# Linear branch of a gated attention mix: transpositions by transposing DMAs in place of TensorE and VectorE, and 107 vector packs spread anew

## The chip, the cores and the metric

The kernel runs on one core of a Trainium2 chip. The metric is the time of one execution in microseconds, measured on the device. The engines are TensorE (PE in the profile), VectorE (DVE), ScalarE (ACT), GpSimd (POOL) and SyncE (SP), which issues most DMAs.

## The reference

Two branches read the same x (2048 tokens, 512 features, bf16, 32 heads of 16) and are mixed by a gate of one number per token.

```python
x = A_x
g = sigmoid((x * gate_w).sum(-1, keepdims=True))
# A: softmax attention
q, k, v = heads(x @ A_wqkv)
a = heads_back(softmax(q @ k.T * 16**-0.5) @ v) @ A_wo
# B: linear attention with softmax features ("hedgehog")
q, k, v = heads(x @ B_wqkv)
pq, pk = q @ w_phi, k @ w_phi                      # 16 x 16 per head
phi_q = concat([softmax(pq), softmax(-pq)], -1)    # 32 features
phi_k = concat([softmax(pk), softmax(-pk)], -1)
kv, z = phi_k.T @ v, phi_k.sum(tokens)
b = heads_back((phi_q @ kv) / (phi_q @ z + 1e-6)) @ B_wo
return g * a + (1 - g) * b
```

## The kernel before

**Units and packs.** The attention branch is cut into 2048 units: one head, one block of 128 keys, one chunk of 512 queries. Four heads make a pack, 16 packs (all key blocks, kt 0 to 15) a group, 32 groups the branch: 512 packs. Scores of a unit are one matmul on a quarter of TensorE's rows (`_scores`, L839) into a PSUM bank. For most units ScalarE takes the exponential (`_exp`, L891), in instructions of 3 and 2 units alternately, out of a ring of five banks. The values follow as matmuls on quarters of TensorE's columns (`_values`, L958), accumulated over a group in one further bank. `_norm` then transposes the group's sums and divides.

**Vector packs.** Some packs ("away") do not go to ScalarE. For these VectorE builds the exponential from bit patterns: four instructions from PSUM (`_vector_bits`, L777, tile va) and three shifted copies (`_vector_terms`, L795, tile vp), so that such a pack has 16 value matmuls instead of 4. `PACKS` says how many packs of each group are away, `CHOICE` which.

**Linear branch.** `_b_fuse` multiplies the projection weights by the feature weights once for K (s=1) and once for Q (s=0): it transposes the weights into WT (TensorE L1050, copy L1055), and the product (L1068) goes back into WB (L1073). `_b_pair` makes the features of two tiles of 128 tokens: projection, a chain of VectorE instructions (L1099 to L1131) and one exponential on ScalarE (L1124). For K they are summed into kv (`_b_kv`, L1148). For Q, `_b_phit` transposes them into phiT: 8 transposes of 128x128 (L1189) and one copy (L1196) a tile. `_b_num` multiplies by kv (L1213), divides (L1220 to L1225, tile nb, two buffers) and transposes the result (L1235, copy L1241) into onTB, which shares its memory with WT. `_b_out` and `_out` add both branches' output products (L1252, L1285) in one bank, and the rows are stored. The branch works in four chunks of 512 tokens.

**The order.** Nothing is issued in program order. `Plan.order` is a list scheduler: every operation has a cost, a latency, a priority (mostly a due time counted in packs) and sometimes a release time. It takes what can start first, the lowest priority among equals, and writes a fixed queue for each engine. Banks outside the ring are handed out as they come free. The constants `K0, SK` and `Q0, SQ` are due times of the K and Q halves in packs (first one, and step per tile); `LEAD`, `FIRST` say how far ahead of its pack a vector pack is begun; `AHEAD` how late other matmuls may run before scores. At low load `pad` and `filler` add matmuls on zeros (L965). On the chip each engine then runs its queue in order, and an operation waits on semaphores for what it needs. DMAs on SP have a semaphore each and also run in the order's sequence.

Of the kernel before, what the change touches and what calls it, by code (L numbers as in the profile page):

```python
# [7 lines left out]
ALU = mybir.AluOpType  # L8
AX = mybir.AxisListType

P = 128
# [32 lines left out]
class Op:  # L44
    def __init__(self, eng, fn, cost, name, prio, rel, kind, lat):
        self.eng, self.fn, self.cost, self.name = eng, fn, cost, name
        self.prio, self.rel, self.kind, self.lat = prio, rel, kind, lat
        self.deps = []
        self.users = []
        self.left = 0  # L50
        self.need = False
        self.acquire = None
        self.release = None
        self.sem = None
        self.start = self.end = None
        self.on_commit = None
        self.array = 0.0
        self.filler = 0
        self.slack = None
        self.fits = True  # L60
        self.pad = False
        self.want = None
        self.tiles = []
        self.filled = 0
# [39 lines left out]
class Plan:  # L104
# [10 lines left out]
    def __init__(self):  # L115
        self.ops = []
        self.now = -1
        self.free_banks = []
        self.keep = None
        self.open = None  # L120
        self.pad = None
        self.grow, self.grow_at = None, 1e9
# [30 lines left out]
    def _bank_for(self, o):  # L153

        free = self.free_banks
        if o.want is not None:
            return [b for b in free if b[0] == o.want]
        if self.now >= self.grow_at - (20 if o.kind == "col" else 2):
            free = [b for b in free if b[0] != self.grow]
        return free if len(free) > (self.keep is not None and self.keep is not o.acquire) else []  # L160

    def order(self):
# [14 lines left out]
        while left:  # L177
# [82 lines left out]
            if o.on_commit:  # L260
                o.on_commit(o)
# [5 lines left out]
        return queues  # L267

# [82 lines left out]
class _Kernel:  # L351
    RING, WIDER = 5, 99999
# [3 lines left out]
    AHEAD = 0.56  # L356
    NB, NVA, NVP, LEAD = 4, 4, 6, 11
    FIRST = 6
    KT0, KTS, NKT = 1, 3, 5
    KEEP, EARLY = 14, 2.5  # L360
# [13 lines left out]
    def build(self):  # L374
        with ExitStack() as ctx:
# [4 lines left out]
            p.grow = self.RING  # L380
# [279 lines left out]
    def _proj_q(self, qc, cp, bank=None):  # L660
        n = qc * 4 + cp
        due = 32 * n - 14.0 if n else -2.0
# [72 lines left out]
    PACKS = (2, 0, 4, 3, 2, 3, 5, 1, 5, 4, 3, 3, 5, 5, 4, 2, 3, 5, 3, 2, 4, 4, 3, 3, 2, 5, 2, 3, 3, 5, 4, 3)  # L735
    CHOICE = ((), (7,), (4, 10), (1, 7, 13), (1, 4, 10, 13), (1, 4, 7, 10, 13))

    def _plan_vector(self):

        self.away = []  # L740
        for g, n in enumerate(self.PACKS):
            self.away += [self.NT * g + k for k in self.CHOICE[n]]
        self.hooks = {}
        hook = lambda p, fn: self.hooks.setdefault(max(0, p), []).append(fn)
        for k, p in enumerate(self.away):
            due = max(p - self.LEAD, self.FIRST)
            past = lambda n: self.away[n] + 1 if n >= 0 else 0
            hook(max(int(due) - 4, past(k - self.NVA)), lambda k=k, p=p, due=due: self._vector_bits(k, p, due))
            hook(max(p - 2, past(k - 1 - (self.NVP - len(SHIFTS)) // len(SHIFTS))), lambda k=k, p=p: self._vector_terms(k, p))
# [4 lines left out]
    def _value_copies(self):  # L754
        end = self.KT0 + self.KTS * (self.NKT - 1) + 1
        self.o_vc = [self.plan.op("DVE", lambda e, cp=cp: e.tensor_scalar(
            self.vc[:, cp], self.V[:, self.KT0:end:self.KTS, cp, :], FACTOR, None, op0=ALU.mult), 0.27,
# [3 lines left out]
    def _vector_bits(self, number, pack, due):  # L761
# [6 lines left out]
        step = 1.0  # L768
        parts = []
        for j in range(self.NB):  # L770
# [8 lines left out]
                op0=ALU.mult, op1=ALU.add), self.c_dve(512), deps=[m] + b.readers, name="v_bits", prio=at - 40,  # L779
# [4 lines left out]
    def _vector_terms(self, number, pack):  # L784
# [5 lines left out]
        for k, (shift, scaled) in enumerate(SHIFTS):  # L790
            x = len(SHIFTS) * number + k
            if x >= self.NVP:
# [3 lines left out]
                         0.07 + n * 0.00026, reads=[b_a], writes=[b], name="v_term", prio=pack - 2)  # L796
            self.terms[pack].append((t, b, scaled))

    def _attention(self):
# [9 lines left out]
        plan.grow_at = self.mine[self.WIDER] / 4 if self.WIDER < len(self.mine) else 1e9  # L809
# [8 lines left out]
        while a < len(self.mine):  # L818
            b = min(a + (2 if a < self.WIDER and len(self.exps) % 2 else 3), len(self.mine))
# [30 lines left out]
    def _ring(self, a):  # L850

        return a % self.RING if a < self.WIDER else (a - self.WIDER) % (self.RING + 1)

    def _qk(self, a, b):
# [17 lines left out]
        def commit(_):  # L872
            plan.now = max(plan.now, (units[-1] + 1) // 4)
        o.on_commit = commit
        o.tiles = [u % 4 for u in units]
        o.pad = k >= 8
        if a == self.WIDER + 3:
            o.acquire, o.want = Job(), self.RING
# [4 lines left out]
    def _exp(self, a, b):  # L883
# [10 lines left out]
        last = range(max(a, len(self.mine) - self.RING - (len(self.mine) > self.WIDER)), b)  # L894
        if last:
            o.on_commit = lambda o: plan.free_banks.extend((self._ring(x), o.end + o.lat, [o]) for x in last)
        self.exps.append(o)

    def _pv(self, p):
# [22 lines left out]
        o = self.plan.op("PE", run, 0.23, reads=[self.b_zero], deps=deps, name=f"pv{p}", prio=p + (2.5 if kt else self.EARLY), kind="col",  # L922
                         acquire=None if kt else ot, array=0.0533 * len(src))
        def commit(_):
            if kt == 0:
                plan.open, plan.keep = ot, None
            elif kt == (self.KEEP if plan.now < plan.grow_at else 99) and g + 1 < self.NPACK // NT and self.ot[g + 1].bank is None:
                plan.keep = self.ot[g + 1]
            elif kt == NT - 1:
                plan.open = None  # L930
        plan = self.plan
        o.on_commit = commit
# [7 lines left out]
    def _pv_terms(self, p):  # L940
# [3 lines left out]
        for tile, buf, scaled in self.terms.pop(p):  # L944
# [5 lines left out]
                             prio=p + 2.6, kind="col", array=0.2133)  # L950
# [23 lines left out]
    def _norm(self, qc, src, side, last, dst, b_dst, due, job, alone=False):  # L974
# [5 lines left out]
           deps=last, writes=[b_T1[side]], name="n_t1", prio=due - 8, release=job)  # L980
        if not (side or alone):
# [6 lines left out]
        op("DVE", lambda e: e.reciprocal(rinv[:, lo:hi], rinv[:, lo:hi]), 0.12 + 0.055 * n, reads=[b_rinv],  # L988
# [3 lines left out]
            rinv[:, lo:hi, :, None].to_broadcast([P, n, 16, 16]), ALU.mult), 0.05 + 0.25 * n,  # L992
# [5 lines left out]
    K0, SK, Q0, SQ = 30.0, 13.25, 226.0, 16.0  # L998

    def _branch_b(self):  # L1000
# [27 lines left out]
        for ch in range(NQC):  # L1028
            for tt in (0, 2):
# [3 lines left out]
                self._b_phit(tt, phi, 0, due + 12)  # L1033
                self._b_phit(tt + 1, phi, 1, due + 14)
# [6 lines left out]
    def _b_fuse(self, s, due):  # L1041
        op = self.plan.op
        for half in range(2):
            job = Job()
            m = None
            for c2 in range(2):
                def tr(e, c=2 * half + c2, c2=c2, job=job):
                    bank = self._bank(job).bitcast(BF16)
                    for cp in range(4):
                        ins = e.transpose(bank[:, 512 * c2 + P * cp:512 * c2 + P * cp + P],  # L1050
                                          self.WB[:, c, D * s + P * cp:D * s + P * cp + P], self.iden[:])
                    return ins
                m = op("PE", tr, 4 * self.c_pe(128), reads=[self.b_WB, self.b_iden], deps=[m] + self.b_WT.readers,
                       name="wtr", prio=due, rel=due - 10, acquire=None if c2 else job)
            o = op("DVE", lambda e, half=half, job=job: e.tensor_copy(  # L1055
                self.WT[:, :, 256 * half:256 * half + 256].rearrange("p q (c m) -> p c q m", c=2),
                self._bank(job).bitcast(BF16).rearrange("p (c q m) -> p c q m", c=2, q=4)), 0.62, deps=[m], name="wtr_ev",
                prio=due, release=job)
            if half:
                self.b_WT.writers, self.b_WT.readers = [first, o], []  # L1060
            first = o
# [120 lines left out]
    def _b_phit(self, tt, slot, k, due):  # L1182
        op = self.plan.op
        job = Job()

        def tr(e):
            bank = self._bank(job).bitcast(BF16)
            for gg in range(8):
                ins = e.transpose(bank[:, P * gg:P * gg + P], self.bq[:, slot, k, P * gg:P * gg + P], self.iden[:])  # L1189
            return ins  # L1190
        if tt == 0:
            self.phit_war = list(self.b_phiT.readers)
            self.b_phiT.writers, self.b_phiT.readers = [], []
        m = op("PE", tr, 8 * self.c_pe(128), reads=[self.b_bq[slot], self.b_iden], deps=self.phit_war, name="phit",
               prio=due, acquire=job)
        o = op("DVE", lambda e: e.tensor_copy(  # L1196
            self.phiT[:, :, tt * TOK:tt * TOK + TOK],
            self._bank(job).bitcast(BF16).rearrange("p (g q) -> p g q", g=8)), 0.605, deps=[m] + self.phit_war,
            name="phit_ev", prio=due, release=job)
        self.b_phiT.writers.append(o)  # L1200

    def _b_num(self, t, due):
# [27 lines left out]
        job = Job()  # L1230

        def tr(e):
            bank = self._bank(job).bitcast(BF16)
            for pr in range(4):
                ins = e.transpose(bank[:, P * pr:P * pr + P], nb[:, P * pr:P * pr + P], self.iden[:])  # L1235
            return ins
        m = op("PE", tr, 4 * self.c_pe(128), reads=[b_nb, self.b_iden], name="nbt", prio=due + 1, acquire=job)
        if tt == 0:
            self.ontb_war = list(self.b_onTB.readers)
            self.b_onTB.writers, self.b_onTB.readers = [], []  # L1240
        self.b_onTB.writers.append(op("DVE", lambda e: e.tensor_copy(  # L1241
            self.onTB[:, :, tt * TOK:tt * TOK + TOK],
            self._bank(job).bitcast(BF16)[:, 0:D].rearrange("p (r q) -> p r q", q=TOK)), 0.34,
            deps=[m] + self.ontb_war, name="nbt_ev", prio=due + 1, release=job))
# [20 lines left out]
    def _out(self, qc):  # L1265
        op, NT, NQC = self.plan.op, self.NT, self.NQC
        for tt in range(4):
            t = 4 * qc + tt
            final = qc == NQC - 1
            due = max(128 * (qc + 1) + 8, self.Q0 + self.SQ * (4 * qc + 4) + 22) + 4 * tt  # L1270
# [71 lines left out]
```

## Time and profile before

| | |
|---|---|
| median of 3 runs | 791.22 us (790.95 to 792.47) |
| profiled execution | 790.92 us |
| its span, first to last instruction | 788.9 us |
| busy: TensorE | 766.6 us, 97% |
| busy: ScalarE | 768.6 us, 97% |
| busy: VectorE | 729.4 us, 92% |
| mean granted TensorE clock | 1.000 |
| DMA: moved in the span | 9.48 MB |

Busy time is the union of an engine's instructions. Matmuls are pipelined and their ends are modelled, so TensorE's share says how often it had work, not how fast it ran. In the tables, "PE" is the matmul and "PEld" its weight load; "SPq" is SP's queue of DMA issues. Durations of neighbouring instructions on VectorE and ScalarE overlap by some 0.1 us, and the chain of waits lists the distances instead.

### The profile page before, as it was taken

What the parts mean: (1) busy time and instruction counts of PE and PEld (TensorE: products, weight loads), DVE (VectorE), ACT (ScalarE), POOL (GpSimd) and SP (SyncE); (2) the same over time, 40 slices, a digit from 0 to 9 for tenths busy, and PEclk for the clock granted to TensorE, in tenths of its full rate; (3) what the DMA queues carried; (4) which work ended last, traced back from release to release, by engine and by line L of the source; (5) the groups of instructions that cost most, each with busy time, mean ns of one, the idle gap of its engine ahead of it and who ended that gap; (6) DMA issues with size and microseconds to landing.
All of it is one profiled execution on the core that took longest, in us unless ns stands there. A gap on an engine that the chain in (4) does not pass through costs nothing.

```text
span 788.9 us, 17147 instructions
## 1 busy us (share of the span) xinstructions
PE 766.6 (97%) x7506; PEld 243.9 (31%) x7506; DVE 729.4 (92%) x1325; ACT 768.6 (97%) x671; POOL 6.9 (1%) x14
## 2 busy tenths in 40 slices
PE   9999999999999999999999999999999999999998
PEld 4333333233222232222222333223332233223332
DVE  5778989898999999999999999899988999799994
ACT  5799999999999999999999999999999999999996
POOL 2000000000000000000000000000000000000000
PEclk9999999999999999999999999999999999999999
DMA  9200000000000000000000000000000000000000
GB/s 267 55 2 1 2 1 2 1 2 1 2 1 2 1 2 1 2 2 1 2 2 1 2 1 8 15 8 1 2 7 21 2 2 2 14 15 1 2 2 27
DMA packets 10857, 9.48 MB, mean 12 GB/s; under 512 B 3616, under 2 KB 10272, under 8 KB 10784
## 3 DMA queue, kind: packets, MB, share of 16 engines
q1 hardware_dynamic: 8912, 7.75, 3.2%
q8 instruction: 58, 0.95, 0.5%
q10 hardware_dynamic: 1872, 0.66, 0.3%
q14 instruction: 15, 0.12, 0.1%
HBM read 6.31 MB, written 2.10 MB: 11 GB/s over the span
## 4 chain that ended last, share of the span: by engine, by line
ACT 81%; DVE 9%; PE 9%; issue 0%
ACT ET L891 78%; ACT bq L1124 3%; DVE va L777 3%; PE ps L839 3%; DVE vp L795 2%; PE ps L958 2%; PE ps L634 1%; PE ps L688 1%; PE ps L1252 1%; PE ps L1285 0%; PE ps L594 0%; PE ps L965 0%; PE ps L609 0%; DVE xT L615 0%; DVE VB L1083 0%; DVE bq L1121 0%
## 5 line engine op out<-in xcount | busy, mean ns | idle before, releaser
L891 ACT ACTIVATE ET<-ps 128x1536 bf16<-128x1536 f32 (+1 forms) x651 | 740.5, 1327 | 11.4 <-PE ps L839 10.4
L839 PE MATMUL ps<-qT,kT 32*128 32x512 bf16 x2048 | 340.2, 384 | 12.7 <-ACT ET L891 8.7
L777 DVE TENSOR_SCALAR va<-ps 128x512 uint16<-128x512 f32 x420 | 276.5, 682 | 6.7 <-PE ps L839 5.9
L795 DVE TENSOR_SCALAR vp<-va 128x2048 uint16<-128x2048 uint16 x315 | 209.0, 686 | 1.3 <-PE ps L958 0.9
L839 PEld LDWEIGHTS ps<-qT,kT 32*128 32x128 bf16 x2048 | 83.9, 91 | 266.6 <-ACT ET L891 145.3
L958 PE MATMUL ps<-ET,V 128*32 128x512 bf16 x1628 | 158.4, 386 | 0.6 <-DVE T L979 0.3
L958 PE MATMUL ps<-vp,vc 128*32 128x512 bf16 x840 | 74.8, 384 | 0.9 <-DVE vp L795 0.9
L965 PE MATMUL ps<-kT,zero 128*32 128x512 bf16 x832 | 75.0, 386 | 0.0
L958 PEld LDWEIGHTS ps<-ET,V 128*32 128x32 bf16 x1628 | 41.3, 94 | 68.8 <-issue 57.0
L634 PE MATMUL ps<-WB,xT 128*128 128x512 bf16 x192 | 54.8, 383 | 0.6 <-DVE T L979 0.2
L958 PE MATMUL ps<-vp,V 128*32 128x512 bf16 x420 | 41.3, 384 | 0.9 <-DVE vp L795 0.9
L958 PE MATMUL ps<-va,V 128*32 128x512 bf16 x420 | 41.7, 387 | 0.0
L634 PE MATMUL ps<-xT,WA 128*128 128x512 bf16 (+1 forms) x132 | 36.8, 377 | 0.4 <-DVE va L777 0.2
L1124 ACT ACTIVATE bq<-bq 128x2048 bf16<-128x2048 bf16 x16 | 31.7, 1983 | 0.0
L958 PEld LDWEIGHTS ps<-vp,vc 128*32 128x32 bf16 x840 | 19.8, 95 | 34.3 <-issue 17.0
L965 PEld LDWEIGHTS ps<-kT,zero 128*32 128x32 bf16 x832 | 18.6, 94 | 36.2 <-issue 34.2
L979 DVE STREAM_TRANSPOSE T<-ps 128x512 f32<-128x512 f32 x32 | 22.7, 708 | 7.4 <-PE ps L958 7.3
L1099 DVE CAST bq<-ps 128x512 bf16<-128x512 f32 x32 | 21.8, 683 | 6.6 <-PE ps L634 6.6
L674 DVE TENSOR_TENSOR qT<-ps,mask 128x1024 bf16<-128x1024 f32 x15 | 18.3, 1217 | 2.8 <-PE ps L634 2.8
L634 PEld LDWEIGHTS ps<-WB,xT 128*128 128x128 bf16 x192 | 12.6, 97 | 24.8 <-issue 12.0
L1294 DVE CAST WB<-ps 128x512 bf16<-128x512 f32 x12 | 8.3, 690 | 12.6 <-PE ps L1285 11.2
L688 PE MATMUL ps<-WA,xT 128*128 128x128 bf16 x256 | 19.6, 220 | 0.0
(84 smaller groups left out, 439.6 us busy)
## 6 DMA issues: line engine op xcount, KB each, us to landing
xn<-in_A_x_dram SPq DMA_DIRECT2D x3, 512.0 KB, 7.1
WB<-in_B_wqkv_dram SPq DMA_DIRECT2D x1, 1536.0 KB, 8.8
out_dram<-WB SPq DMA_DIRECT2D x12, 128.0 KB, 1.7
WA<-in_A_wqkv_dram SPq DMA_DIRECT2D x3, 384.0 KB, 8.8
xn<-in_A_x_dram SPq DMA_DIRECT2D x2, 256.0 KB, 3.7
wphi<-in_B_w_phi_dram SPq DMA_DIRECT2D x32, 0.5 KB, 2.1
WoA<-in_A_wo_dram SPq DMA_DIRECT2D x1, 512.0 KB, 4.1
WoB<-in_B_wo_dram SPq DMA_DIRECT2D x1, 512.0 KB, 5.1
```

The lines of the kernel that those rows point to most:

```text
L634: ins = e.matmul(self._bank(job)[:, 0:n], lhs(c), rhs(c), start=(c == 0), stop=(c == 3))
L674: [lambda e, b: e.tensor_tensor(self.qT[:, s0:s0 + 2, :], b[:, None, :].to_broadcast([P, 2, QCH]), self.mask[:, :, None].to_broadcast([P, ...
L688: ins = e.matmul(self._bank(job)[:, P * tt:P * tt + P], self.xT[:, c, QCH * j + TOK * tt:QCH * j + TOK * tt + TOK], self.WA[:, 2, c, P * c ...
L777: parts.append(op("DVE", lambda e, j=j, job=job: e.tensor_scalar(self.va[:, slot, j, :], self._bank(job), SCALE * LOG2E * 128.0, (127.0 - ...
L795: self.plan.op("DVE", lambda e, t=t, shift=shift: e.tensor_scalar(flat(t), a, float(shift), None, op0=ALU.add), 0.07 + n * 0.00026, reads= ...
L839: return e.matmul(out, self.kT[32 * i:32 * i + 32, cp, kt * TOK:(kt + 1) * TOK], self.qT[32 * i:32 * i + 32, s, :], start=True, stop=True, ...
L891: o = plan.op("ACT", lambda e: e.activation(self.ET[:, a % NS:a % NS + n, :], self.ps[:, self._ring(a):self._ring(a) + n, :], ACT.Exp, sca ...
L958: ins = e.matmul(self._bank(ot)[32 * i:32 * i + 32, :], V[:, v0:v0 + 32], tile, start=(kt == 0), stop=(kt == self.NT - 1), tile_position=( ...
L965: ins = e.matmul(self._bank(ot)[32 * i:32 * i + 32, :], self.zero[:], self.kT[:, 0, 0:QCH], start=False, stop=False, tile_position=(0, 32 ...
L979: op("DVE", lambda e: e.transpose(T1[:, side].rearrange("p b s -> p (b s)"), src()), 0.635, deps=last, writes=[b_T1[side]], name="n_t1", p ...
L1099: [lambda e, b, k=k: e.tensor_copy(bq[:, k].rearrange("p (g s v) -> p g s v", g=8, s=2)[:, :, 0, :], b.rearrange("p (g v) -> p g v", g=8))],
L1124: op("ACT", lambda e: e.activation(flat, flat, ACT.Exp), self.c_act(2048) + 0.045, reads=[b], writes=[b], name="b_exp", prio=due + 1)
```

## The change

1. The three kinds of transposes of the linear branch (weights, Q's features, quotients) are done by DMAs that transpose on the way from SBUF to SBUF, all issued by SP, 8 + 16 + 16 of them. TensorE's transposes and VectorE's copies for them go, with the banks between. In the order each is entered with a cost of 0.3 us on SP and a latency (`TURN`) of 5.0 us.
2. The away packs are listed as bits per group for kt 1, 4, 7, 10, 13 (`AWAY`, 107 in place of 105). Per group they were 2 0 4 3 2 3 5 1 5 4 3 3 5 5 4 2 3 5 3 2 4 4 3 3 2 5 2 3 3 5 4 3 and are 0 2 3 3 3 3 3 3 4 4 5 2 3 4 3 4 5 3 4 3 3 5 2 3 3 4 4 4 3 3 5 4.
3. Constants of the order get other values: due times of the linear branch, lead and priorities of vector packs, of the group's transposition and of output rows. Some costs are entered anew.
4. Code that had no effect at these settings (a wider ring) goes, and callbacks become `_commit`.

```diff
-    RING, WIDER = 5, 99999
+    RING = 5
-    AHEAD = 0.56
-    NB, NVA, NVP, LEAD = 4, 4, 6, 11
-    FIRST = 6
+    AHEAD = 0.53
+    NB, NVA, NVP, LEAD = 4, 4, 6, 12.25
+    FIRST = 3
-    KEEP, EARLY = 14, 2.5
+    KEEP = 12
+    TURN = 5.0
+    STEP, BITS, TERM, PVX, NORM, QDUE, PUT = 0.85, -56.0, 4.5, -0.7, -22, -14.0, 6.95
...
-    PACKS = (2, 0, 4, 3, 2, 3, 5, 1, 5, 4, 3, 3, 5, 5, 4, 2, 3, 5, 3, 2, 4, 4, 3, 3, 2, 5, 2, 3, 3, 5, 4, 3)
-    CHOICE = ((), (7,), (4, 10), (1, 7, 13), (1, 4, 10, 13), (1, 4, 7, 10, 13))
+    AWAY = (0, 20, 25, 13, 11, 22, 22, 14, 30, 15, 31, 10, 21, 29, 13, 27, 31, 28, 29, 14, 26, 31, 5, 25, 14, 15, 15, 30, 21, 21, 31, 23)
...
-            hook(max(int(due) - 4, past(k - self.NVA)), lambda k=k, p=p, due=due: self._vector_bits(k, p, due))
+            hook(max(min(int(due) - 4, p - 2), past(k - self.NVA)), lambda k=k, p=p, due=due: self._vector_bits(k, p, due))
...
-        step = 1.0
+        step = self.STEP
...
-                op0=ALU.mult, op1=ALU.add), self.c_dve(512), deps=[m] + b.readers, name="v_bits", prio=at - 40,
+                op0=ALU.mult, op1=ALU.add), self.c_dve(512), deps=[m] + b.readers, name="v_bits", prio=at + self.BITS,
...
-                         0.07 + n * 0.00026, reads=[b_a], writes=[b], name="v_term", prio=pack - 2)
+                         0.07 + n * 0.00026, reads=[b_a], writes=[b], name="v_term", prio=pack + self.TERM)
...
-                             prio=p + 2.6, kind="col", array=0.2133)
+                             prio=p + self.PVX, kind="col", array=0.2133)
...
-           deps=last, writes=[b_T1[side]], name="n_t1", prio=due - 8, release=job)
+           deps=last, writes=[b_T1[side]], name="n_t1", prio=due + self.NORM, release=job)
...
-    K0, SK, Q0, SQ = 30.0, 13.25, 226.0, 16.0
+    K0, SK, Q0, SQ = 23.0, 12.65, 203.5, 16.8
...
     def _b_fuse(self, s, due):
...
+        war = self.b_WT.readers
+        self.b_WT.writers, self.b_WT.readers = [self._turn(
+            f"wt{s}{c}", self.WT[:, :, P * c:P * c + P], self.WB[:, c, D * s:D * s + D], [self.b_WB], war, due, due - 10)
+            for c in range(4)], []
...
+    def _turn(self, name, out, src, reads, deps, due, rel=-99):
+
+        return self.dma("SP", name, lambda e: e.dma_start_transpose(out, src), cost=0.3, reads=reads, deps=deps, prio=due,
+                        rel=rel, lat=self.TURN)
+
+    def _b_phit(self, t, slot, k, due):
+        if t % 4 == 0:
             self.phit_war = list(self.b_phiT.readers)
             self.b_phiT.writers, self.b_phiT.readers = [], []
...
+        self.b_phiT.writers.append(self._turn(
+            f"ph{t}", self.phiT[:, :, t % 4 * TOK:t % 4 * TOK + TOK], self.bq[:, slot, k, :], [self.b_bq[slot]],
+            self.phit_war, due))
...
+        self.b_onTB.writers.append(self._turn(
+            f"nb{t}", self.onTB[:, :, tt * TOK:tt * TOK + TOK], nb, [b_nb], self.ontb_war, due + 1))
...
-            due = max(128 * (qc + 1) + 8, self.Q0 + self.SQ * (4 * qc + 4) + 22) + 4 * tt
+            due = max(128 * (qc + 1) + 8, self.Q0 + self.SQ * (4 * qc + 4) + 22) + self.PUT * tt
```

## The prediction

> **What bounds the kernel now.** I read the page first: the busy shares, then the chain of work that ended last, then the costliest groups.
>
> ```profile
> span 788.9 us, 17147 instructions
> PE 766.6 (97%) x7506; PEld 243.9 (31%) x7506; DVE 729.4 (92%) x1325; ACT 768.6 (97%) x671; POOL 6.9 (1%) x14
> ACT 81%; DVE 9%; PE 9%; issue 0%
> L891 ACT ACTIVATE ET<-ps 128x1536 bf16<-128x1536 f32 (+1 forms) x651 | 740.5, 1327 | 11.4 <-PE ps L839 10.4
> L777 DVE TENSOR_SCALAR va<-ps 128x512 uint16<-128x512 f32 x420 | 276.5, 682 | 6.7 <-PE ps L839 5.9
> L795 DVE TENSOR_SCALAR vp<-va 128x2048 uint16<-128x2048 uint16 x315 | 209.0, 686 | 1.3 <-PE ps L958 0.9
> ```
>
> PE and ACT are both busy 97%, but the chain settles which of them sets the end: ACT holds 81% of it. TensorE's 97% also contains 208 fillers of 4 matmuls (L965, 832 records) that compute nothing, and its weight loads waited 145.3 us for ACT's exponentials, so it has room. VectorE at 92% has less, and in the 20 us windows from 200 to 460 us it is busy 19.3 us or more in each.
>
> In the chain in order of time ACT runs unbroken for most of the span. I read two of its pieces, one early and one late, to get the pace:
>
> ```profile
> 314.82 50.64 ACT ET L891 x45
> 705.42 66.89 ACT ET L891 x59
> ```
>
> The second column is the length. The pieces give 1.125 and 1.134 us per exponential, against 740.5/651 = 1.137 us over the whole kernel. So the steady state is close to ACT's own speed, and at most (1.137 - 1.125) x 651 = 7.9 us of small stalls can be recovered there. The other idle time of ACT is in the head. I read ACT's timeline from 20 to 36 us (the bracket is idle time before the row):
>
> ```profile
> 30.62 2.36 ACT L891 ACTIVATE ET<-ps 128x1536 bf16<-128x1536 f32 x2 [3.02 <-PE ps L839]
> 34.61 2.37 ACT L891 ACTIVATE ET<-ps 128x1536 bf16<-128x1536 f32 x2 [1.63 <-PE ps L839]
> ```
>
> ACT starves for 3.02 + 1.63 = 4.65 us because scores are missing. Behind that, the chain shows why: K's last quarter waits for VectorE, where terms of vector packs stand between the copies of x and K.
>
> ```profile
> 26.78 1.29 DVE xT L615 x2
> 28.07 1.21 DVE vp L795 x2
> 29.27 0.62 DVE kT L657
> 29.89 1.73 DVE vp L795
> 31.62 0.59 DVE kT L657
> 32.22 0.61 DVE vp L795
> ```
>
> The three vp pieces are 1.21 + 1.73 + 0.61 = 3.55 us.
>
> **The packs (ACT).** PACKS sums to 105; the bits set in AWAY are 107. Each pack is 4 units of 512 columns that leave ACT. 512 packs x 4 - 420 = 1628 units now, 1620 after. 740.5/1628 = 0.455 us per unit, times 8: **-3.6 us**, on the path, since nothing else covers ACT.
>
> **The head.** Group 0 loses both its packs (AWAY[0] is 0); the first one to go is pack 23. That takes the 3.55 us of vp out from between the copies, and gives ACT 8 units, 8 x 0.455 = 3.6 us of work, to do while it would have starved. Either nearly closes the 4.65 us, both do: **-4.6 us**.
>
> The same stretch gets a new wait. Four transposing DMAs per weight half replace TensorE's transposes (L1050) and VectorE's copies (L1055), and everything else on SP is ahead of them: its timeline shows the 32 small weight transfers until 28.55 us, then WoA and WoB until 29.57. K0 goes from 30 to 23, so the product that needs them (L1068, first at 45.1 us) is due 7 packs earlier, 7 x 788.9/512 = 10.8 us: 34.3 us. Four issues at 0.44 to 0.53 us (SP's rows for single transfers) end at 31.6. From there the landing lies between 1.7 us (128 KB stores of the output) and 5.1 us (WoB, which is in front on the same DMA engines): 33.3 to 36.7, a wait of 0 to 2.4 us for TensorE. Queued behind it, in TensorE's fixed order, are the scores, and ACT holds about one scored group in hand, 1.1 us. I take **+1.5 us**, nearer to the upper end because the loads in front are certain.
>
> **VectorE, TensorE and banks.** Gone are the copies L1196 (16, 10.8 us busy), L1241 (16, 6.6) and L1055 (4, 2.8): 20.2 us. New are 2 packs of 4 bit operations at 276.5/420 = 0.658 and 3 terms at 209.0/315 = 0.663: 9.2 us. Net -11.0 us on VectorE, off ACT's path. TensorE loses 128 + 64 + 32 = 224 transposes (18.8 us busy) and gains 24 value matmuls at 158.4/1628 = 0.097 us (2.3 us). Of the three PSUM banks outside the scores' ring, 36 uses go and 8 come. What this returns is part of the 7.9 us. Score loads (L839) waited 25.8 + 7.8 = 33.6 us for vector packs' work against 145.3 us for ACT, so 33.6/178.9 = 19% of the stalls are VectorE's: **-1.5 us**; the bounds are +3.2 (crowding, below) and -7.9.
>
> **The landings of the other transposes.** 16 transfers of 256 KB (features) and 16 of 128 KB (products) go onto SP, which issues nothing between 29.6 us and the first store at 490 us. After that, a transposition can stand behind a store that waits for its copy, at 0.33 us per issue and with stores 5 us or more apart. No transposing DMA is in this trace. Nearest rows: 128 KB stores land in 1.7 to 2.1 us, 256 KB loads in 3.7, and the slowest rows need 8.8. The order is laid out for 5.0 us, 5.6 for the second of a pair. I take 3.7, the row of the same size, so nothing is late: **0**. Its cover: between the end of the fourth features copy of a chunk and the first numerator matmul (L1213) now lie 12.5, 3.1, 16.4 and 16.1 us, and between a product tile and the multiply that overwrites its buffer 11.5 us (457.5 to 469.0). Here a rule of the Trainium skill speaks against the change. "VectorE: DVE Perf Modes", section "The three transpose paths", gives 390 ns for a 128x128 block on TensorE and 1309 ns by the DMA crossbar, and says to use TensorE where PSUM will do; no row of this trace shows the second figure. Eight blocks one after the other would be an estimated 10.5 us; the sum by that is given with the rivals.
>
> **The tail.** From the end of the last exponential (781.3 us) to the end of the span 7.6 us pass, in value matmuls, output products and stores. The last vector pack stays at 13 of group 31. The last chunk's numerators come due at 203.5 + 16.8 x 16 = 472.3 instead of 482, farther from the end. 0. One pack more in each of groups 30 and 31 falls where VectorE is busy 13.9 of 20 us (760 to 780).
>
> **Sum.** 788.9 - 3.6 - 4.6 + 1.5 - 1.5 = 780.7 us span. The profiled execution took 790.92 us, 2.0 more than its span, and the median of the runs is 0.3 above it: **783.0 us**.
>
> **Rivals.**
> *Only the packs count* (787.6). The head starves as before for another reason (x or the gate's products), and the freed VectorE time buys nothing: 791.2 - 3.6. For it: VectorE holds only 9% of the chain. A milder form is crowding: the last K pair (due 200.1) and the first Q pair (203.5) come 3.4 packs, 5.2 us, apart, where they were 10.5 packs apart. One pair costs VectorE 8.4 us (its rows from L1099 to L1131 added up), so 3.2 us are late once: 786.2.
>
> *Late landing* (slower). The crossbar handles a transfer's blocks less densely than a plain copy, and 256 KB need as long as the slowest row of this trace, 8.8 us, 128 KB half. The second transfer of a feature pair then lands at 17.6, 12.0 after the order expects it; less 3.1 of cover and 1.1 in ACT's hand, the second chunk stalls 7.8 us. The two weight halves (17.6 against 4 x 0.3 + 5.0 = 6.2, cover 0.5 and 2.6) stall 9.8 and 7.7. With 25.3 us in place of my 1.5 the time is 806.8. In general, for a landing L the three places add 6L - 27.5, so it decides from L = 6.2 us, where the gain of 8.2 is used up. Against it: 3.7 us for a plain 256 KB, with all 16 DMA engines otherwise idle. By the skill's 1309 ns a block the same formula, with 1.7 for the first chunk, gives an estimated 818.
>
> *It doesn't do what it says*: the transposes cannot fail to move, as the instructions are replaced one for one; only their landing is open.
>
> **How the numbers follow.** The forecast (778 to 786.2, with 783.0 as its middle) has 0.57; only the packs, crowding included, 0.17 (786.2 to 789.6); cases in between, in which a part of a landing eats the gain, 0.07; late landing 0.19. A measurement of this kernel tells about 0.2%, 1.6 us, from no change, so faster is 0.57 + 0.17 = 0.74, same 0.07, slower 0.19. The low end, 777.5, is the forecast without the new wait and with half of the 7.9 us recovered (783.0 - 1.5 - 4.0); below it I leave 0.04. The high end, 793, takes in the beginning of the late landings and leaves 0.16 above.
>
> **What would show it.** Right: L891 at 648 instructions and near 736 us; no idle time of ACT over 1.5 us after its first exponential until the tail; L1196, L1241, L1055 gone and VectorE near 718 us; transposes of 256 KB landing in under 5 us; no matmul of L1213's or L1252's kind waiting long for a DMA. Wrong: rows of TensorE or VectorE waiting for a DMA on phiT, WT or nb, several us each; a landing above 6.2 us; a gap of ACT between 30 and 40 us as long as before; or more small stalls in the steady state, seen as more than 1.14 us per exponential.

## The result and the profile after

The changed kernel takes 794.87 us (median of 14 runs, 792.02 to 802.65) against 791.05 us before (14 runs, 790.59 to 792.47): ratio 1.0065, 95% interval 1.0045 to 1.0085. It is slower by 0.65%, clear of the scatter but less than 2%; the forecast was 783.0, which is faster than before. The spread comes with the clock: the mean granted TensorE clock of its runs lies between 0.992 (792.0 us) and 0.976 (802.7 us).

The page of the changed kernel, profiled in a run of 794.79 us, the lines that answer to those of before:

```profile
span 793.0 us, 16713 instructions
PE 754.2 (95%) x7238; PEld 238.1 (30%) x7304; DVE 720.6 (91%) x1303; ACT 766.9 (97%) x668; POOL 6.9 (1%) x14
ACT 79%; DVE 8%; PE 7%; SPq 4%; issue 1%; DMA 0%
L894 ACT ACTIVATE ET<-ps 128x1536 bf16<-128x1536 f32 (+1 forms) x648 | 738.4, 1299 | 17.2 <-PE ps L846 16.1
```

The exponentials (now L894) are 648 as expected, but their busy time falls only from 740.5 to 738.4 us, and the idle time before them grows from 11.4 to 17.2. Together that is +3.7 us of the span's +4.1. New in the chain is SPq with 4%: the queue of DMA issues. ACT's timeline from 20 to 52 us shows where (idle time before each row in brackets):

```profile
18.61 13.92 ACT L894 ACTIVATE ET<-ps 128x1536 bf16<-128x1536 f32 x12
37.78 1.45 ACT L894 ACTIVATE ET<-ps 128x1536 bf16<-128x1536 f32 x1 [5.25 <-PE ps L846]
39.83 1.02 ACT L894 ACTIVATE ET<-ps 128x1024 bf16<-128x1024 f32 x1 [0.59 <-PE ps L846]
...
49.56 3.71 ACT L894 ACTIVATE ET<-ps 128x1536 bf16<-128x1536 f32 x3 [1.04 <-PE ps L846]
```

The old gaps (3.02 and 1.63 us) are gone: ACT runs unbroken to 32.5 us. Then it stands for 5.25 us, and for 12 us after that every exponential waits again, 0.2 to 1.3 us each (4.3 us in all). The chain in order of time says what the first gap is (start, length, what):

```profile
29.19 0.51 SPq L516
29.74 1.29 SPq L1171
31.08 1.32 SPq L1171
32.44 1.27 SPq L1171
33.75 2.50 DMA WT<-WB
36.61 0.58 PE ps L1055 x4
```

SP issues WoB's load until 29.7 us. Then come the four transposing DMAs of K's weights (L1171), the first three holding SP for 1.3 us each; the fourth begins at 33.75 and lands at 36.25, and the fused product (L1055) can start. TensorE's own timeline has its last score at 30.93 us and then this row:

```profile
36.61 0.58 PE L1055 MATMUL ps<-bq,WT 128*128 128x128 bf16 x4 [5.29 <-DMA WT<-WB]
```

The second part of the loss is in the windows of 2 us; after each engine's busy time stand the granted clock, the DMA share and GB/s:

```profile
30.00:32.00 2.00, 1.32 (x9) 0.38 (x8) 2.00 (x4) 2.00 (x3) 1.16 (x1) 1.00 0.66 219
32.00:34.00 2.00, 0.00 (x0) 0.00 (x0) 0.28 (x1) 0.54 (x1) 0.00 (x0) 0.58 1.14 351
34.00:36.00 2.00, 0.00 (x0) 0.00 (x0) 0.00 (x0) 0.00 (x0) 0.00 (x0) 0.50 1.02 205
...
48.00:50.00 2.00, 2.00 (x10) 0.47 (x9) 0.69 (x1) 0.96 (x2) 0.00 (x0) 0.65 0.33 66
50.00:52.00 2.00, 2.00 (x15) 0.51 (x13) 1.48 (x3) 2.00 (x3) 0.00 (x0) 1.00 0.00 0
```

TensorE's last matmul ends at 31.3 us. At 32.3, 1.0 us later, its granted clock drops to half, and it stays there until about 49.4. The windows add up to 17.1 us at half clock: 1.7 in the one at 32, 14 in the seven that follow, 1.4 in the one at 48. From 36.6 us on TensorE is busy again, yet ACT starves, because the scores come too slowly.

In the list of waits no engine waits for the other 32 transposing DMAs. Their rows in the list of DMA issues (count, us to landing in the median):

```profile
phiT<-bq SPq DMA_TRANSPOSE x16, 3.2
WT<-nb SPq DMA_TRANSPOSE x16, 2.4
```

### The profile page after: what moved, and what is told of

It is laid out like the page before. It is cut to its first block, busy times and chain, and to the rows that moved or that the text cites. A ratio compares the mean times of both kernels' runs of the same rounds, so it can differ in the third digit from the quotient of the medians.

```text
span 793.0 us, 16713 instructions
## 1 busy us (share of the span) xinstructions
PE 754.2 (95%) x7238; PEld 238.1 (30%) x7304; DVE 720.6 (91%) x1303; ACT 766.9 (97%) x668; POOL 6.9 (1%) x14
## 4 chain that ended last, share of the span: by engine, by line
ACT 79%; DVE 8%; PE 7%; SPq 4%; issue 1%; DMA 0%
ACT ET L894 76%; ACT bq L1111 3%; PE ps L846 3%; DVE va L785 3%; DVE vp L803 2%; PE ps L960 2%; SPq L549 2%; PE ps L967 1%; PE ps L867 1%; SPq L495 1%; SPq L1171 0%; DVE T L981 0%; SPq L510 0%; DMA WT<-WB 0%; DVE bq L1086 0%
## 5 line engine op out<-in xcount | busy, mean ns | idle before, releaser
L894 ACT ACTIVATE ET<-ps 128x1536 bf16<-128x1536 f32 (+1 forms) x648 | 738.4, 1299 | 17.2 <-PE ps L846 16.1
L960 PE MATMUL ps<-vp,vc 128*32 128x512 bf16 x856 | 77.2, 384 | 0.9 <-DVE vp L803 0.5
L967 PE MATMUL ps<-kT,zero 128*32 128x512 bf16 x784 | 70.2, 393 | 0.0
L642 PE MATMUL ps<-WB,xT 128*128 128x512 bf16 x176 | 51.7, 383 | 2.5 <-issue 2.1
L642 PE MATMUL ps<-xT,WA 128*128 128x512 bf16 (+1 forms) x112 | 32.5, 381 | 3.9 <-issue 2.4
L960 PEld LDWEIGHTS ps<-vp,vc 128*32 128x32 bf16 x856 | 21.5, 95 | 32.4 <-issue 13.6
L1108 DVE TENSOR_TENSOR bq<-bq,btree 128x2048 bf16<-128x2048 bf16 x16 | 19.4, 1214 | 0.1
L1118 DVE TENSOR_TENSOR bq<-bq,brec 128x2048 bf16<-128x2048 bf16 x16 | 19.3, 1207 | 0.0
```

Of the source, the lines that this page charges most:

```text
L642: ins = e.matmul(self._bank(job)[:, 0:n], lhs(c), rhs(c), start=(c == 0), stop=(c == 3))
L894: o = plan.op("ACT", lambda e: e.activation(self.ET[:, a % NS:a % NS + n, :], self.ps[:, self._ring(a):self._ring(a) + n, :], ACT.Exp, sca ...
L960: ins = e.matmul(self._bank(ot)[32 * i:32 * i + 32, :], V[:, v0:v0 + 32], tile, start=(kt == 0), stop=(kt == self.NT - 1), tile_position=( ...
L967: ins = e.matmul(self._bank(ot)[32 * i:32 * i + 32, :], self.zero[:], self.kT[:, 0, 0:QCH], start=False, stop=False, tile_position=(0, 32 ...
L1108: + [("b_sub", two(2048), lambda e: e.tensor_tensor(x, x, spread(tree[:, :, 0]), ALU.subtract))],
```

## The experiments

Theory A: the weights' landing makes TensorE wait, and the half clock that follows costs as much again; the rest of the change does what was forecast. Theory B: the DMAs of the second half, or the new order, cost the time all along.

**The weights' transposes undone** (`weights_back`).

```diff
 def _b_fuse(self, s, due):
-        self.b_WT.writers, self.b_WT.readers = [self._turn(f"wt{s}{c}", ...) for c in range(4)], []
+        # TensorE's transposes and VectorE's copies, as in the kernel before
```

> The changed kernel with one part undone: the weights' transposes are TensorE's again (with VectorE's copies), features and products stay with the DMAs, all constants and packs as changed. Theory A (the weights' landing at 31 to 37 us makes TensorE wait 5.3 us, and the half clock that follows it until 49 us costs about as much again): the gap of ACT at 32 us goes, the clock stays 1.00 there, 782 to 786 us. Theory B (the 32 transposing DMAs of the second half, or the new order, cost the time all along): 791 us or more, as the changed kernel.

784.93 us (784.61 to 786.73), ratio 0.9921 (0.9903 to 0.9940). ACT's timeline has no gap, and in the windows of 20 us (columns as above) the clock stays whole:

```profile
23.23 27.39 ACT L894 ACTIVATE ET<-ps 128x1536 bf16<-128x1536 f32 x24
```

```profile
20.00:40.00 20.00, 19.08 (x200) 8.12 (x199) 13.34 (x22) 19.99 (x19) 1.33 (x1) 1.00 0.18 55
40.00:60.00 20.00, 19.96 (x180) 7.45 (x179) 14.97 (x25) 20.00 (x20) 0.00 (x0) 1.00 0.00 2
```

Taking 8 of the 40 DMAs back made a difference of 9.9 us. The 32 DMAs of the second half are still there, and so are the new constants, so theory B falls.

**The order told the truth about SP** (`sp_told`). By the costs in its code the order let SP reach the first of the four DMAs at 21.7 us, had them land by 27.9 and placed the first product at 30.9; SP reached the first DMA at 29.7.

```diff
-                self.WA[...], ..., prio=prio, lat=lat)
+                self.WA[...], ..., prio=prio, lat=lat, cost=2.0 if eng == "SP" and prio > -46 else 0.5)
-        o = self.plan.op("SP", parts, 0.45 * len(parts), ...)
+        o = self.plan.op("SP", parts, (0.53 if len(parts) > 4 else 0.78) * len(parts), ...)
-  _turn: cost=0.3
+  _turn: cost=1.3
```

> The changed kernel, all transposes by DMA, but the order is told what SP's issues really take: 2.0 us for two loads of the A weights, 0.78 for a gate column, 0.53 for a small weight block, 1.3 for a transposing DMA (it assumed 0.5, 0.45, 0.45 and 0.3). Theory A: the first fused product is placed after the landing, the gap at 32 us and the half clock go, 782 to 786 us. Theory B: 791 us or more.

The first fused product starts at 40.57 us, after the landing, and the gap is gone, with all transposes by DMA. In the three runs at a mean clock of 1.000 the time is 784.6 to 784.9 us, the same as `weights_back`. The other nine take 787.9 to 790.4 at 0.991 to 0.995 (median of all 789.71, ratio 0.9964, 0.9945 to 0.9983), so the median misses the 782 to 786 that A expected. A holds for the head, and there is a second way to lose the clock. The profiled run shows it (windows of 4 us):

```profile
308.00:312.00 4.00, 3.14 (x11) 0.53 (x10) 3.85 (x7) 3.24 (x4) 0.00 (x0) 0.74 0.02 4
312.00:316.00 4.00, 4.00 (x26) 0.70 (x24) 1.95 (x5) 2.60 (x3) 0.00 (x0) 0.50 0.00 0
316.00:320.00 4.00, 4.00 (x24) 0.65 (x23) 2.87 (x5) 3.42 (x3) 0.00 (x0) 0.50 0.00 0
320.00:324.00 4.00, 4.00 (x31) 0.70 (x28) 3.44 (x5) 2.63 (x3) 0.00 (x0) 0.56 0.00 0
```

From 307.8 us TensorE issues single scores that wait for VectorE (bit operations and the group's transposition), with pauses of no more than 0.3 us between them, and at 309.9 the clock halves for 13.6 us. The DMA engines are busy 0.02 of that window.

**Busy while waiting** (`busy_wait`). The wait stays, but TensorE works in it.

```diff
+            if s and not c:
+                def busy(e, job=job):          # issued before the wait for the DMAs
+                    for _ in range(24):
+                        e.matmul(self._bank(job), self.kT[:, 0, 0:P], self.kT[:, 0, 0:QCH], start=True, stop=True)
...
```

> The changed kernel with 24 full matmuls of 512 columns, about 5.1 us, that TensorE runs into the bank of the first fused product just before it waits for the weights' landing; they are overwritten. The wait for the data stays, TensorE is not idle in it. If the idle time is what halves the clock (theory A): the clock stays 1.00 from 20 to 60 us, ACT's gap of 5.3 us stays, about 5 us less than the changed kernel, 787 to 791 us. If the clock fell for another reason (the DMAs' traffic): 0.50 as before, 794 to 802 us.

TensorE's timeline, and the windows of 20 us:

```profile
31.74 5.34 PE L1071 MATMUL ps<-kT 128*128 128x512 bf16 x24
36.92 0.39 PE L1063 MATMUL ps<-bq,WT 128*128 128x128 bf16 x4
```

```profile
20.00:40.00 20.00, 19.48 (x171) 8.20 (x169) 9.02 (x15) 15.22 (x15) 1.32 (x1) 1.00 0.32 80
40.00:60.00 20.00, 20.00 (x163) 6.39 (x159) 15.15 (x23) 20.00 (x19) 0.00 (x0) 1.00 0.15 28
```

The DMAs move as much as in the changed kernel (80 and 27 GB/s in these two windows there), and ACT's gap stays (4.77 us), but the clock is 1.00. Four runs at a mean clock of 1.000 take 788.9 to 789.1 us; the median of all is 789.82, and others lost some of the clock (up to 804.62 us at 0.977), the profiled one at 604 us. The changed kernel's profiled run (794.8, clock 0.987) is 5.8 us above 789.0, with 20.5 us at half clock (17.1 in the head and 3.4 at 456 us); its fastest run (792.0, 0.992) is 3.0 above. That is the price of the half clock. From 789.0 to the 784.9 of `weights_back`, 4 us, is the price of the wait itself.

**The DMAs alone** (`dma_alone`). The kernel before with the three `_turn` calls, all else as it was.

> The kernel before with the transposing DMAs alone (latency 5.0, issue 0.3 in the order), its own 105 packs and constants. Its order puts the first fused product 8 us later than the changed kernel does. Theory A: the landing at about 36 us is before that, no wait of over 1 us, clock 1.00: 787 to 791 us, the DMAs themselves cost nothing. Theory B: 794 us or more.

792.06 us (791.18 to 794.33), ratio 1.0013 (0.9999 to 1.0028): between what the two theories expected, 1.1 us above A's range and no different from the kernel before. TensorE waits for no DMA, the clock is 1.00 in the profiled run; the old gap in the head stays:

```profile
30.88 2.37 ACT L892 ACTIVATE ET<-ps 128x1536 bf16<-128x1536 f32 x2 [3.03 <-PE ps L840]
34.25 15.98 ACT L892 ACTIVATE ET<-ps 128x1536 bf16<-128x1536 f32 x14 [1.01 <-PE ps L840]
```

VectorE's busy time falls from 729.4 to 710.2 us, and nothing comes of it.

**The order alone** (`order_alone`). All three kinds of transposes back on TensorE and VectorE, new packs and constants.

> The changed kernel with all three kinds of transposes on TensorE and VectorE again; packs and constants as changed. If the new packs and constants bring the gain by themselves (3.6 us of ACT's work, 4.6 of head gap): 783 to 787 us, as with the weights' transposes alone undone. If they need the VectorE time and the banks that the DMAs free: VectorE is 15 us fuller, ACT waits more in the steady state, 790 us or more.

797.0 to 818.1 us (clock 0.998 to 0.969); even the fastest run is 5.9 us above the kernel before. In its profile, the fastest run, VectorE is 15.6 us fuller than in the changed kernel, and ACT has waits of 2.7, 1.1 and 5.3 us at 496, 557 and 685 us and one of 6.0 in the tail (3.7 before). So neither half of the change gained anything without the other. Whether the cause is VectorE's load, the banks, or only that these due times were chosen for the other order, this run doesn't separate.

**Two packs fewer** (`two_less`), from `weights_back`.

```diff
-    AWAY = (0, 20, 25, 13, 11, 22, 22, 14, 30, 15, 31, 10, 21, 29, 13, 27, 31, ...
+    AWAY = (0, 20, 25, 13, 11, 22, 22, 14, 30, 15, 27, 10, 21, 29, 13, 27, 27, ...
```

> The kernel with the weights' transposes on TensorE (784.9 us), with 105 packs away: group 10 and group 16 keep their pack at 10. The prediction's term for two packs is 3.6 us of ACT's work: 788.5 us (787.5 to 790). If VectorE's load decides, it gets no slower: 785 us or less.

789.36 us; in the five runs at full clock 788.0 to 789.2, in the median 788.4, some 3.6 above `weights_back`. The term for the packs stands.

**Packs in group 0** (`head_packs`), from `two_less`: `AWAY` begins with 10 (packs 4 and 10) in place of 0.

> The same kernel with 107 packs, of which two are at 4 and 10 of group 0, as in the kernel before, in place of one in each of groups 10 and 16. If the packs in group 0 make the head's gap (the prediction's 4.6 us): ACT again waits 3 to 5 us between 25 and 36 us and the time is 788 to 791 us. If the gap has another cause: no gap, 785 us.

796.55 us (794.08 at full clock). The gap is back, 1.05 and 3.99 us:

```profile
24.05 5.54 ACT L894 ACTIVATE ET<-ps 128x1024 bf16<-128x1024 f32 x5 [1.05 <-PE ps L846]
33.59 17.38 ACT L894 ACTIVATE ET<-ps 128x1536 bf16<-128x1536 f32 x15 [3.99 <-PE ps L846]
```

The time rose further than the expected 788 to 791: behind the head this order has another gap of 2.42 us at 74 us and smaller ones after it.

**More fillers everywhere** (`told_filled`), from `sp_told`: `SHARE = 0.62`.

> All transposes by DMA, SP's issues told to the order, and the fillers' share of TensorE's time (SHARE) at 0.62 in place of 0.6. In 9 of 12 runs the kernel without it lost its clock for 13.7 us or so. If that is too little work on TensorE in a stretch (since 224 transposes went): the clock stays 1.00 in most runs and the spread shrinks to under 2 us, at 785 to 789 us. If the clock falls for another reason: spread of 5 us as before.

788.3 to 801.8 us, clock 0.997 to 0.977: the spread grew, which neither case expected. The run settles nothing: another share shifts the whole order, and with it the thin places (in the profiled run the clock fell at 642.6 us, not at 310). Hence the next one, in which the order stays.

**Fillers in the thin place** (`thin_filled`), from `sp_told`.

```diff
             p.finals = self.stores
+            for o in p.queues["PE"]:           # after the order is fixed
+                if o.filler and 184 <= int(o.name[2:]) <= 212:
+                    o.filled += 1
```

> The kernel with all transposes by DMA and SP's issues told (sp_told), in the very same order of work; only in packs 184 to 212 one filler of 4 matmuls on zeros more goes before each value matmul of ScalarE's packs. In the profile of sp_told TensorE waited for VectorE there between single scores (307.8 to 310.2 us) and its clock halved at 309.8 for 13.7 us. If thin work on TensorE makes the clock fall: no half clock near 310 us, most runs at 1.00, median 785 to 786.5 us in place of 789.7. If the clock falls for another reason: 789 to 790.5 us as before.

```profile
308.00:312.00 4.00, 3.57 (x34) 0.82 (x22) 3.15 (x6) 3.22 (x3) 0.00 (x0) 1.00 0.00 0
312.00:316.00 4.00, 4.00 (x44) 0.98 (x40) 4.00 (x9) 3.91 (x4) 0.00 (x0) 1.00 0.00 0
```

All six runs have a clock of 0.998 or more, where 9 of 12 had lost it: thin work made it fall. But the time is 788.45 us, 3.6 above the full-clock runs of `sp_told`, where 785 to 786.5 were expected. In its profile ACT waits seven times for scores between 308 and 348 us, 2.3 us in all; that the fillers delay the scores in the same queue is the likely reason, not shown by a profile of `sp_told` at full clock. The smaller spread is bought with much of the gain.

**More packs** (`packs_109`), from `weights_back`: 109 packs away, `Q0, SQ = 199.87, 16.51`, `TERM` 3.66, `QDUE` -13.67, `PUT` 6.51.

> The kernel with the weights' transposes on TensorE (784.9 us), with 109 packs away in place of 107 and due times moved a little (Q0 199.87, SQ 16.51, TERM 3.66, PUT 6.51). If ACT's work is the bound and VectorE, 20 us of whose copies went, still has room: two packs less for ACT are 3.6 us, 779 to 782 us. If VectorE is full: 784 us or more.

781.33 us (781.22 to 782.67), ratio 0.9876 (0.9863 to 0.9890): the fastest version here, 9.8 us below the kernel before. ACT's 3.6 us came off again.

## Why the prediction was wrong, point by point

**The packs, -3.6: right.** 648 exponentials, and 3.6 us between 105 and 107 packs (`two_less` against `weights_back`; ACT's busy time for them 741.0 and 737.5).

**The head's gap, -4.6: right.** It is gone where group 0 has no packs and back where it has. ACT's idle time before its exponentials fell from 11.4 to 7.1 us in `weights_back`, by 4.3.

**The new wait in the head, +1.5: here it failed.** The place and the data were right. The landing, 33.3 to 36.7 forecast and 36.25 measured, was right by luck in part: the four issues were to end at 31.6, but the fourth only began at 33.75, and it landed 2.5 us after that. The other end was wrong. The product was expected at 34.3 us, from the shift of a due time. But a due time only ranks what is ready; the order starts an operation when it believes its data there. It had the weights landed at 27.9 us and placed the product at 30.9, and TensorE was free for it at 31.3. The term, 0 to 2.4 us of wait, measured 5.3 us of wait and 4.1 us of time. The issues were priced from plain DMAs at 0.44 to 0.53 us; a transposing one holds SP for 1.2 to 1.3.

**What was not in the sum at all: the clock.** The profile before shows 1.00 throughout, and a wait of TensorE was priced by its length. The half clock that came of it cost 3.0 us in the fastest run and 5.8 in the profiled one, about as much as the wait. The Trainium skill, "TensorE: Matmul & The Clock Gate", says in Part 1 that the gate watches TensorE's activity in windows of 3413 ns and passes half the pulses after an idle window. The length agrees with these traces: 17.1 us is five such windows, 13.6 us four. The condition does not: the clock fell 1.0 us after the last matmul had ended, and in `sp_told` it fell with no pause over 0.3 us, so no idle window had passed. The remedy that the Trainium skill gives on that page, to keep TensorE from idling for a window, is what `busy_wait` did, and it held the clock in the head. That a stretch with work, but little of it, is enough (11 matmuls in the 4 us in which it fell, 34 where it did not) was shown by `sp_told` and `thin_filled`.

**The steady state, -1.5: wrong.** Without the wait the forecast is 781.5, and `weights_back` measured 784.9. VectorE's net relief was near the estimate (729.4 to 720.6, -8.8 for -11.0), but nothing came back for it; `dma_alone` frees 19 us of VectorE for nothing. There was nothing to come back. The 7.9 us of small stalls, of which the term was a part, came from 740.5 us over 651 exponentials; but 740.5 is busy time, and busy time holds no wait. ACT's waits before were these (us in total, times, longest):

```profile
ACT ET L891 <- PE ps L839: 10.4, 3, 5.7
ACT xT L1291 <- PE ps L1285: 3.7, 1, 3.7
ACT L891 <- issue: 2.4, 1, 2.4
ACT ET L891 <- PE ps L958: 0.8, 1, 0.8
```

The first row is 5.7 us at the very start and the two gaps in the head; the second is the tail, the third the start. Between head and tail 0.8 us was left. The 33.6 us for vector packs were waits of TensorE, and reading their share as time of ACT was the error. ACT had a scored group in hand meanwhile: in the changed kernel it ran on for 1.2 us after the last score. Of the 3.4 us that `weights_back` lies above the forecast, 1.5 are this term and 1.3 are two new waits of ACT for VectorE before exponentials of features (L1126). What the freed time is worth is more packs, 1.8 us each, as `packs_109` shows; whether the kernel before had room for them without the DMAs, in an order made for it, was not run.

**The whole.** 781.5 + 3.4 (steady state and the two waits) + 4.1 (the wait for the weights) + 5.8 (the half clock) = 794.8, the profiled run.

**The other landings, 0: right.** 3.2 us for 256 KB where 3.7 was taken, 2.4 for 128 KB, none above 4.6, all inside the 5.0 of the order. In these rows four further blocks of 128x128 cost 3.2 - 2.4 = 0.8 us, 0.2 a block; a time near 1.3 us is what an issue holds SP. By the Trainium skill's 1309 ns for a block ("VectorE: DVE Perf Modes", section "The three transpose paths") eight would have taken an estimated 10.5 us; the measured 3.2 does not bear that out.

**The tail, 0: right** (7.7 us from the last exponential for 7.6).

**The rivals.** Late landing was the rival with the right place and the wrong reason: the time went through SP's queue and a believed time, not through the crossbar. *Only the packs count* was right that the freed VectorE time buys nothing, and wrong that the head starves as before.

What stays open is where exactly the limit of thin work lies, and which orders come near it: the clock losses of single runs after 60 us were traced in one profile each.

## What to carry to other kernels

In a kernel whose order is fixed by a planner, ask of each operation that is moved to a DMA queue what the queue is doing at that time and when the planner believes the data there: its consumer starts at the believed time, and behind it waits everything on its engine. Price a wait of TensorE with the clock that it may lose, which here cost as much as the wait and spread the runs. Time freed on an engine off the critical path was worth nothing here until work of the bound engine was moved onto it, so cost the two together. Before you count on small stalls of the bound engine, look for them in its own list of waits.

## What the runs showed of the hardware

In the changed kernel a transposing DMA from SBUF to SBUF held SP for 1.19 to 1.37 us in most cases, 2.4 at most, where a plain store held it for 0.33; it landed 2.4 us (128 KB) or 3.2 us (256 KB) after its issue began, in the median, and 5.1 at most. TensorE's clock halved for 17.1, 13.6 and 3.4 us at a time, once 1.0 us into a pause of 5.3 us and otherwise in stretches where it never stopped for long but had little to do; how often this happened differed from run to run of the same kernel (clock 0.976 to 0.992).
